# Two attention-and-FFN chunks, products of zeros between the real ones: adding them in chunk 1

## The chip, the core and the metric

The kernel runs on one core of one Trainium2 chip. The metric is the device time of the whole program in microseconds; the time before is the median of three runs. The profile shows one execution: for each engine when its instructions ran and what they waited for, and for TensorE (PE) also the clock that it was granted, 1.00 being full speed.

## The reference

Four batches of 768 tokens with 8 heads of 64 go through a sparse attention and then through a feed-forward block. In the attention a query sees the keys closer than 16 positions and, beside them, 24 block summaries: the maximum of 32 keys, and the mean of 32 values.

```python
k_sum = k.reshape(B, H, nb, block, D).max(axis=3)
v_sum = v.reshape(B, H, nb, block, D).mean(axis=3)
scores_l = scale * np.matmul(q, k.transpose(0, 1, 3, 2))     # masked: |i-j| < 16
scores_s = scale * np.einsum('bhsd,bhnd->bhsn', q, k_sum) + np.log(block)
a = softmax(concat([scores_l, scores_s]))                    # (written out in full there)
x = a @ concat([v, v_sum])                                   # heads side by side: (B, S, 512)
h = np.maximum(x @ w_in, 0.0)                                # 512 -> 1024
conv_out = sum over k of conv_w[k] * h shifted by k - 1      # three taps along the tokens
out = (h * sigmoid(conv_out)) @ w_out                        # 1024 -> 512
```

## The kernel before

**Chunks and units.** A chunk is half a batch, 384 tokens; there are eight, `c` = 0 to 7, and batch 0 is chunks 0 and 1. The feed-forward width of 1024 is cut into eight row blocks of 128. A unit `(c, u)` does row block `u` of chunk `c`, and with it a slice of the attention of the next chunk, so that attention and feed-forward share PE.

**The products, all on PE.** Attention: `pq` (L260, scores), `pt` (L308, transposing the weights), `xp` (L329, weights times values), `pv` (L234, one transpose for the value means). Feed-forward: `f1` (L404), 12 products of 384 or 386 columns for a row block, from three pairs of parts (`win_hi` with `xh`, `win_hi` with `xl`, `win_lo` with `xh`); and `f2` (L473), the last product. One `f2` tile is 128 tokens by 512 outputs; it adds up eight parts, `fc` = 0 to 7, of three products each (`wout_hi` with `ghi`, `wout_lo` with `ghi`, `wout_hi` with `glo`), in one PSUM bank. Then ScalarE (ACT) copies the bank out (`ob`, L482). The parts are `[fc]` lists that `work(c)` deals out over the units: chunk 1 gets the tiles (0,0) and (0,1), 16 parts, over its units 3 to 7 (`EARLY_AT` = 3).

**Behind a row block.** `gate_conv` takes the relu (ACT, L422) and the taps (ACT L425, VectorE (DVE) L434) from the bank of `f1`; `gate_mul` follows with tanh (ACT L451), the gating (DVE L452), `ghi` (ACT L455) and `glo` (GpSimd (POOL) L456). `f1` has three banks.

**Weights of the last product.** Each of the eight row blocks of `w_out` is decoded on ACT (L97) and DVE (L100, L101, L104), then ACT makes `wout_hi` (L127) and POOL makes `wout_lo` (L128). `OUT_AT` puts these splits into the units from (0,6) to (1,4).

**Products of zeros.** `idle` is a bf16 tile of zeros. `warm(where)` issues `WARM[where]` products of 512 columns of it into the PSUM tile `pw` (L78), whose values nobody reads. In chunk 0 that happens at the start, behind attention products and, with `after`, behind the last `f1` product of each unit (three each). `pw` has the tag `f2` with one buffer, so it holds the same bank as the tiles (b, 0), (b, 1) and so on of the last product: the first of them, (0,0), gets the bank when the last product into `pw` has been issued.

**Who sets the order.** From chunk 2 on PE's order is the order of the program (`manual_schedule`, with `ORDERED` = 2). In chunks 0 and 1 a planner sets it, on every engine: it plays the program through with estimated durations and issues on each engine, of what is ready, what stands first in the program. Work that stands later is pulled ahead where the planner sees the engine without other work. All queues run in the order so fixed.

Of the kernel before, what the change touches and what calls it, by code (L numbers as in the profile page):

```python
# [16 lines left out]
P = 128  # L17
# [12 lines left out]
NFC = DF // P  # L30
# [10 lines left out]
EARLY_IN = 2  # L41

OUT_AT = (6, 7, 8, 9, 10, 10, 11, 12)
WARM = {"start": 10, "pq0": 5, "pq1": 12, "pq2": 3, "pq3": 3, "tr": 2, "av": 3, "unit": 3}
EARLY_AT = 3
ORDERED = 2
NGROUP = NCHUNK * NP * 2
# [3 lines left out]
def attention_ffn(ctx, tc, qT, kT, vT, v4, w_in, cwT, w_out, mask8, ident_in, out):  # L51
    nc = tc.nc
# [18 lines left out]
    idle = cp.tile([P, 512], mybir.dt.bfloat16, name="idle")  # L71
# [3 lines left out]
    def warm(where, after=None):  # L75
        def go():
            for i in range(WARM.get(where, 0)):
                nc.tensor.matmul(pw, idle[:, :P], idle, start=True, stop=True)  # L78

        if after is None:  # L80
            go()
        else:
            with tc.issue_after(after):
                go()
# [28 lines left out]
    def split_in(fc, t):  # L113
        weights(t, flat(win_hi, fc), flat(win_lo, fc), f"i{fc}")

    def load_out(fc):
        t = sp.tile([P, 1024], U32, tag="stage", name=f"wo{fc}", bufs=2)
        nc.sync.dma_start(t, w_out[fc].bitcast(U32))
        return t

    def split_out(fc, t):
        weights(t, wout_hi[:, fc, :], wout_lo[:, fc, :], f"o{fc}")
# [18 lines left out]
    def ins(x):  # L141
        return getattr(x, "ins", x)
# [216 lines left out]
    def slot(j):  # L359

        if j % 2 == 0:
            n = j // 2 + 2
            if NP <= n < npair:
                load_k(*divmod(n, NP))
                load_vt(*divmod(n, NP))
            if NP <= j // 2 < npair:
                load_vm(*divmod(j // 2, NP))
            if j // 2 < npair:
                qk(*divmod(j // 2, NP))
        else:  # L370
            n = (j + 1) // 2
            if NP <= n + 1 < npair:
                load_q(*divmod(n + 1, NP))
            if n < npair:
                c, p = divmod(n, NP)
                if c:
                    vmean_pair(c, p)
                    load_v(c, p)
                prep_pair(c, p)

    def slot_t(j):
        if 0 <= j - DEPTH < NGROUP:
            tr(j - DEPTH)

    def slot_av(j):
        n = j - DEPTH - 2
        if n % 2 == 0 and 0 <= n < NGROUP:
            av(n // 2)
# [4 lines left out]
    def f1(c, fc, ccs):  # L393
        hf = c % 2
        n = CH + 2 * hf
        xh, xl = xT[c]
        if ccs[0] == 0:
            f1ps[(c, fc)] = ps.tile([P, 512], F32, tag="f1", name=f"f1_{c}_{fc}", bufs=3)
        ph = f1ps[(c, fc)]
        for cc in ccs:  # L400
            for m, (w, x) in enumerate(
                ((win_hi, xh), (win_hi, xl), (win_lo, xh))
            ):
                last = nc.tensor.matmul(  # L404
                    ph[:, :n],
                    w[:, fc, cc, :],
                    x[:, cc, :n],
                    start=(cc == 0 and m == 0),
                    stop=(cc == NCC - 1 and m == 2),
                )  # L410
        return last
# [3 lines left out]
    def gate_conv(c, fc):  # L415


        hf = c % 2
        n = CH + 2 * hf
        ng = CH - 1 + 2 * hf  # L420
        h = f1ps.pop((c, fc))
        nc.scalar.activation(h[:, :n], h[:, :n], AF.Relu)  # L422
        t = sp.tile([P, CH + 2], F32, tag="t", name=f"t{c}_{fc}", bufs=3)[:, :ng]
        if c in TAP_ACT:
            nc.scalar.activation(t, h[:, hf : hf + ng], AF.Copy, scale=cw[:, fc, 1:2])  # L425
        else:
            nc.vector.tensor_scalar(
                t, h[:, hf : hf + ng], cw[:, fc, 1:2], 1.0, ALU.mult, ALU.mult
            )
        for k in (0, 2):  # L430

            i0 = max(0, 1 - hf - k)
            i1 = min(ng, n - (hf + k - 1))
            nc.vector.scalar_tensor_tensor(  # L434
                t[:, i0:i1],
                h[:, hf + k - 1 + i0 : hf + k - 1 + i1],
                cw[:, fc, k : k + 1],
                t[:, i0:i1],
                ALU.mult,
                ALU.add,  # L440
            )
        held[(c, fc)] = h, t
# [19 lines left out]
    def f2(b, st, fcs, tag="f2", bufs=1):  # L462
        if fcs[0] == 0:
            f2ps[(b, st)] = ps.tile([P, 512], F32, tag=tag, name=f"f2_{b}_{st}", bufs=bufs)
        po = f2ps[(b, st)]
        ss = slice(st * P, (st + 1) * P)
        ghi, glo = gated["hi"], gated["lo"]
        for fc in fcs:
            contracted.add((b, st, fc))
            for m, (gx, w) in enumerate(  # L470
                ((ghi, wout_hi), (ghi, wout_lo), (glo, wout_hi))
            ):
                nc.tensor.matmul(  # L473
                    po,
                    gx[:, fc, ss],
                    w[:, fc, :],
                    start=(fc == 0 and m == 0),
                    stop=(fc == NFC - 1 and m == 2),
                )
        if fcs[-1] == NFC - 1:  # L480
            ob = sp.tile([P, DM], F32, tag="wu", name=f"ob{b}_{st}", bufs=3)
            nc.scalar.activation(ob, po, AF.Copy, scale=0.5)  # L482
            nc.scalar.dma_start(out[b, ss, :], ob)
# [71 lines left out]
    def rooms():  # L555
        gated["hi"] = cp.tile([P, NFC, S], F32R, name="ghi", tag="big_a")
        gated["lo"] = cp.tile([P, NFC, S], F32R, name="glo", tag="big_b")

    def gates(lag):

        while len(pending) > lag:
            c, fc = pending[0]
            b, hf = divmod(c, 2)
            old = (0, 1, 2) if hf == 0 else (2, 3, 4, 5)
            if b and not all((b - 1, st, fc) in contracted for st in old):
                return
            pending.pop(0)
            gate_mul(c, fc)

    def unit(c, u, pieces, together):  # L570


        j = 8 * (c + 1) + 1 + DEPTH + u
        last = c == NCHUNK - 1
        slot(j)
        if together:
            slot_av(j)
            slot_t(j)
        if c == 0 and u < 2:
            for fc in (4 + 2 * u, 5 + 2 * u):  # L580
                split_in(fc, raws[fc])
        if c == 0 and u == 2:
            rooms()
        gates(1)
        early = c == 0 and u < EARLY_IN
        if not early:
            f1(c, u, [0, 1])
        if not together:
            slot_t(j)
        done = f1(c, u, [3] if early else [2, 3])  # L590
        if c == 0:
            warm("unit", ins(done))
        gate_conv(c, u)
        pending.append((c, u))
        assert len(pending) <= 2
        if not together:
            slot_av(j)
        for x in pieces[u]:
            f2(*x)
        if last:  # L600
            gates(0)
        at = NFC * c + u
        for fc in range(NFC):
            if OUT_AT[fc] == at:
                split_out(fc, raws["o", fc])
        for fc in range(NFC):
            if OUT_AT[fc] == at + 1:
                raws["o", fc] = load_out(fc)

    for c in range(NCHUNK):  # L610
        pieces = work(c)
        if c < ORDERED:
            for u in range(NFC):
                unit(c, u, pieces, False)
        else:
            with tc.manual_schedule(engines={mybir.EngineType.PE}):
                for u in range(NFC):
                    unit(c, u, pieces, True)

    for pair in ((2, 3), (4, 5)):  # L620
        for fs in (range(NFC // 2), range(NFC // 2, NFC)):
            for st in pair:
                for fc in fs:
                    f2(B - 1, st, [fc], "f1" if st % 2 else "f2", 3 if st % 2 else 1)
# [55 lines left out]
```

## Time and profile before

| | us |
|---|---|
| three runs | 404.59, 408.15, 409.48 |
| median | 408.15 |
| the profiled execution, its own time | 408.03 |
| its span, first to last instruction | 406.2 |
| PE busy | 386.4 (95%) |
| DVE / ACT / POOL busy | 261.3 / 254.2 / 151.6 |
| mean granted clock of PE | 0.986 |

Between the span and the execution's own time lie 1.83 us that no instruction of the program fills. A busy share is the mean over very different stretches: chunk 0 begins after a stage of attention alone, chunk 1 is roughly the stretch from 80 to 129 us, chunk 7 ends near 381 us, and the last four tiles of the last product follow by themselves. PE works in a pipeline, so what one product costs is read from start to start, not from its duration.

### The profile page before, as it was taken

How to read it: one execution, taken by the hardware profiler on the slowest of the kernel's cores; microseconds unless marked ns; L12 is line 12 of the kernel's file. 1: busy time of each engine (PE TensorE's matmuls, PEld its weight loads, DVE VectorE, ACT ScalarE, POOL GpSimd, SP SyncE). 2: the span in 40 equal slices, each digit the busy share in tenths (PEclk: the TensorE clock that was granted, in tenths of full speed). 3: DMA queues.
4: the chain of work that ended last, by engine and by line, in shares of the span. 5: the costliest groups of instructions: out<-in, count | busy, mean ns of one | idle time of the engine just before them, and what ended most of it. 6: DMA issues, size and time to landing. Idle time of an engine off the chain costs nothing.

```text
span 406.2 us, 8829 instructions
## 1 busy us (share of the span) xinstructions
PE 386.4 (95%) x3164; PEld 319.5 (79%) x3173; DVE 261.3 (64%) x777; ACT 254.2 (63%) x806; POOL 151.6 (37%) x179
## 2 busy tenths in 40 slices
PE   7978869999799999999999999999999999999996
PEld 3546657886678888888888888888788888999884
DVE  4899789998965765668765456466565665556200
ACT  3664799998777677766565777756655654343211
POOL 2327464585953333322432333333332242222200
PEclk9999699999989999999999999999999999999999
DMA  8999863766966774646332344334220000000011
GB/s 290 327 361 211 230 177 115 248 202 192 252 162 205 235 217 123 190 145 192 78 92 78 80 111 112 104 96 117 67 63 28 27 2 26 26 27 26 28 52 52
DMA packets 60715, 54.47 MB, mean 134 GB/s; under 512 B 24640, under 2 KB 51328, under 8 KB 60672
## 3 DMA queue, kind: packets, MB, share of 16 engines
q1 hardware_dynamic: 56928, 47.19, 41.3%
q10 hardware_dynamic: 3744, 6.73, 4.5%
q8 instruction: 25, 0.41, 0.4%
q14 instruction: 18, 0.15, 0.1%
HBM read 45.55 MB, written 6.29 MB: 128 GB/s over the span
## 4 chain that ended last, share of the span: by engine, by line
PE 68%; ACT 11%; DVE 10%; DMA 3%; issue 3%; POOL 3%; SPq 0%; ACTq 0%; DVEq 0%; POOLq 0%
PE f L404 26%; PE f L473 26%; PE pq L260 5%; ACT a L288 5%; PE xp L329 4%; PE pt L308 4%; DVE t L434 3%; PE pw L78 2%; ACT t L451 1%; DMA kw<-kT 1%; DMA k_xh<-kT 1%; ACT f L422 1%; DVE t L452 1%; POOL wout_lo L128 1%; ACT t L425 1%
## 5 line engine op out<-in xcount | busy, mean ns | idle before, releaser
L456 POOL TENSOR_TENSOR glo<-t,ghi 128x383 fp32r<-128x383 f32 (+1 forms) x64 | 66.6, 1041 | 116.3 <-ACT ghi L455 111.8
L434 DVE SCALAR_TENSOR_TENSOR t<-f,cw,t 128x382 f32<-128x382 f32 (+3 forms) x128 | 78.8, 616 | 23.5 <-ACT t L425 20.7
L404 PE MATMUL f<-xh,win_hi 128*128 128x384 f32 (+1 forms) x256 | 93.0, 363 | 0.9 <-ACT win_hi L127 0.9
L404 PE MATMUL f<-xl,win_hi 128*128 128x384 f32 (+1 forms) x256 | 87.7, 343 | 0.0
L404 PE MATMUL f<-xh,win_lo 128*128 128x384 f32 (+1 forms) x256 | 86.9, 340 | 0.0
L473 PE MATMUL f<-wout_lo,ghi 128*128 128x512 f32 x192 | 76.1, 396 | 3.1 <-POOL wout_lo L128 3.1
L288 ACT ACTIVATE a<-a,nm 128x120 f32<-128x120 f32 x192 | 73.3, 384 | 9.1 <-DVE nm L278 8.8
L473 PE MATMUL f<-wout_hi,ghi 128*128 128x512 f32 x192 | 76.3, 398 | 0.2 <-ACT ob L482 0.2
L473 PE MATMUL f<-wout_hi,glo 128*128 128x512 f32 x192 | 75.1, 392 | 0.0
L451 ACT ACTIVATE t<-t 128x383 f32<-128x383 f32 (+1 forms) x64 | 33.6, 525 | 60.4 <-DVE t L434 59.3
L300 POOL TENSOR_TENSOR a<-a,sm 128x360 f32<-128x360 f32 x56 | 45.8, 839 | 64.4 <-DVE sm L297 36.5
L452 DVE SCALAR_TENSOR_TENSOR t<-t,f 128x383 f32<-128x383 f32 (+1 forms) x64 | 35.3, 552 | 28.2 <-ACT t L451 28.2
L404 PEld LDWEIGHTS f<-xh,win_hi 128*128 128x128 f32 x256 | 48.7, 190 | 3.6 <-issue 1.3
L404 PEld LDWEIGHTS f<-xl,win_hi 128*128 128x128 f32 x256 | 49.0, 191 | 0.9 <-issue 0.3
L404 PEld LDWEIGHTS f<-xh,win_lo 128*128 128x128 f32 x256 | 48.8, 191 | 0.2
L278 DVE CUSTOM_DVE_ANT_0 a<-pq,mask 128x120 f32<-128x120 f32 x192 | 42.7, 276 | 1.9 <-PE pq L260 1.9
L473 PEld LDWEIGHTS f<-wout_lo,ghi 128*128 128x128 f32 x192 | 36.3, 189 | 9.7 <-POOL wout_lo L128 4.1
L455 ACT CAST ghi<-t 128x383 fp32r<-128x383 f32 (+1 forms) x64 | 32.6, 509 | 16.6 <-DVE t L452 15.9
L473 PEld LDWEIGHTS f<-wout_hi,glo 128*128 128x128 f32 x192 | 36.2, 188 | 7.7
L473 PEld LDWEIGHTS f<-wout_hi,ghi 128*128 128x128 f32 x192 | 36.1, 188 | 7.3 <-issue 0.6
L308 PE MATMUL pt<-ident,a 128*120 128x128 f32 x192 | 34.0, 285 | 5.4 <-ACT aT L315 3.7
L260 PEld LDWEIGHTS pq<-kw,q 64*64 64x64 f32 x768 | 23.9, 134 | 18.6 <-issue 13.0
(59 smaller groups left out, 505.8 us busy)
## 6 DMA issues: line engine op xcount, KB each, us to landing
va<-v SPq DMA_DIRECT2D x32, 288.0 KB
kw<-kT SPq DMA_DIRECT2D x28, 288.0 KB
q<-qT SPq DMA_DIRECT2D x32, 192.0 KB
out_dram<-ob ACTq DMA_DIRECT2D x24, 256.0 KB
kT<-kT SPq DMA_DIRECT2D x12, 392.0 KB
vt<-vT SPq DMA_DIRECT2D x12, 384.0 KB
wo<-w_out SPq DMA_DIRECT2D x8, 512.0 KB
raw_a<-w_in SPq DMA_DIRECT2D x6, 512.0 KB
```

What stands on the lines that cost most here:

```text
L260: last = nc.tensor.matmul(pq[h][half * QB : (half + 1) * QB, i * NK : (i + 1) * NK], st["q"][r, blk * QB : (blk + 1) * QB], st["kw"][r, bl ...
L278: nc.vector.tensor_tensor_reduce(a[:, i, :], pq[h][:, i * NK : (i + 1) * NK], mask[:, hf, i, :], -0.125, 3.0e38, ALU.add, ALU.min, nm[:, h ...
L288: nc.scalar.activation(a[:, i, :], a[:, i, :], AF.Exp, bias=nm[:, h, i : i + 1], scale=-1.0, accum_out=sm[:, h, i : i + 1],)
L300: (nc.gpsimd if n >= NP else nc.vector).tensor_tensor(a, a, sm[:, h, :].unsqueeze(2).to_broadcast([P, 3, NK]), ALU.mult)
L308: last = nc.tensor.transpose(pt[:NK, i * P : (i + 1) * P], a[:, i, :], ident)
L404: last = nc.tensor.matmul(ph[:, :n], w[:, fc, cc, :], x[:, cc, :n], start=(cc == 0 and m == 0), stop=(cc == NCC - 1 and m == 2),)
L434: nc.vector.scalar_tensor_tensor(t[:, i0:i1], h[:, hf + k - 1 + i0 : hf + k - 1 + i1], cw[:, fc, k : k + 1], t[:, i0:i1], ALU.mult, ALU.add,)
L451: nc.scalar.activation(t, t, AF.Tanh, scale=0.5)
L452: nc.vector.scalar_tensor_tensor(t, t, 1.0, h[:, hf : hf + ng], ALU.add, ALU.mult)
L455: nc.scalar.copy(hi, t)
L456: nc.gpsimd.tensor_tensor(gated["lo"][:, fc, d0 : d0 + ng], t, hi.bitcast(F32), ALU.subtract)
L473: nc.tensor.matmul(po, gx[:, fc, ss], w[:, fc, :], start=(fc == 0 and m == 0), stop=(fc == NFC - 1 and m == 2),)
```

## The change

Two things are added, both on PE, and both change no value. Behind the last `f1` product of the units (1,0), (1,1) and (1,2), `warm("unit")` is now called as in chunk 0: three products of zeros into `pw` each, nine in all. And in `f2`, for the tiles (0,0) and (0,1), each part but the last is followed by two products of zeros that are added to the tile's own bank (`start=False, stop=False`): 7 parts of 2 tiles by 2, 28 in all. With the nine, `pw` is in use up to unit (1,2).

```diff
-WARM = {"start": 10, "pq0": 5, "pq1": 12, "pq2": 3, "pq3": 3, "tr": 2, "av": 3, "unit": 3}
+WARM = {"start": 10, "pq0": 5, "pq1": 12, "pq2": 3, "pq3": 3, "tr": 2, "av": 3, "unit": 3, "part": 2}
@@ f2, in the loop over the parts, behind the three products
+            if (b, st) in ((0, 0), (0, 1)) and fc < NFC - 1:
+
+                for _ in range(WARM["part"]):
+                    nc.tensor.matmul(po, idle[:, :P], idle, start=False, stop=False)
@@ unit
         done = f1(c, u, [3] if early else [2, 3])
-        if c == 0:
+        if c == 0 or (c == 1 and u < EARLY_AT):
             warm("unit", ins(done))
```

## The prediction

> **What bounds the kernel now.** I read the page's first two parts, then the granted clock over all of the span in stretches, then PE's waits in chunk 1, then the timeline of PE around the longest of them and the chain that leads to it. The page and the list of cores:
>
> ```profile
> core 0: 406.2 us, clock 0.986
> PE 386.4 (95%) x3164; PEld 319.5 (79%) x3173; DVE 261.3 (64%) x777; ACT 254.2 (63%) x806; POOL 151.6 (37%) x179
> PEclk9999699999989999999999999999999999999999
> ```
>
> PE is the bound as a whole, and its clock is below full in two slices only, the fifth and the twelfth. Stretches chosen around these two and around chunk 1 (columns: busy time of PE, weight loads, DVE, ACT, POOL with counts, the granted clock, DMA share, GB/s):
>
> ```profile
> 43.50:49.95 6.45, 6.45 (x28) 5.10 (x27) 5.16 (x19) 4.19 (x20) 2.43 (x3) 0.50 0.76 208
> 60.00:88.00 28.00, 27.79 (x285) 22.40 (x287) 26.47 (x80) 25.93 (x88) 16.59 (x21) 1.00 0.56 176
> 88.00:97.80 9.80, 9.80 (x75) 7.87 (x74) 8.60 (x19) 8.77 (x26) 6.75 (x7) 1.00 0.74 226
> 97.80:110.40 12.60, 9.37 (x64) 6.88 (x62) 12.60 (x32) 10.57 (x31) 9.67 (x9) 1.00 0.81 223
> 111.40:114.65 3.25, 3.25 (x25) 2.50 (x24) 1.25 (x4) 2.47 (x11) 0.20 (x1) 0.50 0.94 182
> 114.70:122.50 7.80, 7.64 (x72) 5.88 (x70) 5.75 (x21) 5.55 (x15) 5.23 (x5) 0.99 0.62 168
> 122.50:131.00 8.50, 8.50 (x46) 7.12 (x46) 4.91 (x9) 6.35 (x21) 3.79 (x5) 1.00 0.62 188
> 131.00:381.00 250.00, 248.18 (x2041) 217.70 (x2039) 151.70 (x448) 152.94 (x479) 80.77 (x99) 1.00 0.33 93
> ```
>
> From 60 to 97.8 us PE is full at full clock, and from 122.5 on it is full to the end. Between lies the only soft place of chunk 1: from 97.8 to 110.4 PE is idle for 12.60 - 9.37 = 3.23 us while DVE is busy throughout, and just behind it the clock stands at 0.50 for 3.25 us. What PE waits for there:
>
> ```profile
> PE f L473 <- POOL wout_lo L128: 3.1, 3, 2.4
> 107.40 0.40 PE L473 MATMUL f<-wout_hi,ghi 128*128 128x512 f32 x1
> 107.64 0.34 PE L404 MATMUL f<-xl,win_hi 128*128 128x386 f32 x1
> 110.41 0.50 PE L473 MATMUL f<-wout_lo,ghi 128*128 128x512 f32 x1 [2.44 <-POOL wout_lo L128]
> ```
>
> The sixth part of tile (0,0) stops PE for 2.44 us in its middle, between its first and its second product, until POOL has made the low half of that weight block. The chain that leads there:
>
> ```profile
> 89.50 2.31 PE f L404 x12
> 92.78 0.12 PE pv L234
> 94.02 0.58 ACT t L425
> 96.22 0.98 DVE wu_o L101
> 100.86 0.63 ACT wout_hi L127
> 104.74 1.98 POOL a L300 x2
> 108.67 1.69 POOL wout_lo L128
> ```
>
> It leaves PE behind the row block (1,2) and the transpose `pv`, and runs for 17 us over ACT, DVE and POOL. So products on PE between 93 and 107 us are not on the path, and what delays (1,2) or `pv` is.
>
> **The price of a product of zeros.** A unit of chunk 0 with three of them between `f1` and `pq`, and a place in chunk 1 where `pq` follows `f1` directly; then two products of a part in the dense stretch:
>
> ```profile
> 73.54 0.34 PE L404 MATMUL f<-xh,win_lo 128*128 128x384 f32 x1
> 73.72 0.82 PE L78 MATMUL pw<-idle 128*128 128x512 bf16 x3
> 74.47 0.85 PE L260 MATMUL pq<-kw,q 64*64 64x120 f32 x24
> ...
> 81.96 0.34 PE L404 MATMUL f<-xh,win_hi 128*128 128x386 f32 x1
> 82.22 0.63 PE L260 MATMUL pq<-kw,q 64*64 64x120 f32 x14
> ...
> 127.31 0.39 PE L473 MATMUL f<-wout_hi,ghi 128*128 128x512 f32 x1
> 127.54 0.40 PE L473 MATMUL f<-wout_lo,ghi 128*128 128x512 f32 x1
> ```
>
> From `f1` to `pq` it is 74.47 - 73.54 = 0.93 us with three and 82.22 - 81.96 = 0.26 without: 0.67 for three, 0.22 each. A real product of the same 512 columns follows the last in 0.23, so I take 0.225 also for those added to the tile's bank, which the trace of before does not have. That price has a floor of 0.22 and, if the change of weights between a part and its zeros broke the pipeline, a ceiling of their whole duration, about 0.39 as for the products beside them. Below nothing it can't be: a product holds PE. I take the low end because in the rows above zeros stand between real products and cost no more than that. All 37 cost 9 x 0.223 + 28 x 0.225 = 8.3 us of PE; the question is how much of it lies in idle time.
>
> **Nine behind the row blocks.** Those of (1,0) and (1,1) stand in the full stretch, ahead of (1,2): +1.34 us on the chain's start. There is something against it. The bank of `pw` passes to tile (0,0) only behind the zeros of (1,2), so the tile's first part can no longer run ahead of that row block, as it does now:
>
> ```profile
> 87.98 0.50 PE L473 MATMUL f<-wout_hi,ghi 128*128 128x512 f32 x1
> 88.88 0.62 PE L260 MATMUL pq<-kw,q 64*64 64x120 f32 x6
> 89.43 0.45 PE L404 MATMUL f<-xh,win_hi 128*128 128x386 f32 x1
> ...
> 92.29 0.50 PE L473 MATMUL f<-wout_hi,ghi 128*128 128x512 f32 x1
> 92.62 0.27 PE L234 MATMUL pv<-ident,vs 128*24 128x128 f32 x1
> ...
> 87.71 0.55 DVE L452 SCALAR_TENSOR_TENSOR t<-t,f 128x383 f32<-128x383 f32 x1
> ```
>
> That part takes 88.88 - 87.98 = 0.90 us there, and goes to a place behind (1,2), which is the third row block of 386 columns, the one that starts at 89.43. Whether (1,2) then starts 0.90 earlier depends on its bank: the gating of chunk 0's last block reads a bank of `f1` until 87.71 + 0.55 = 88.26 us, and with PE 1.34 later that is no hindrance. So (1,2) ends 1.34 - 0.90 = 0.44 later. Its own three zeros, issued behind its last product and ahead of `pv`, add 0.67: the chain is 1.1 us late. The bounds: 0.4 (the planner puts `pv` ahead of them, or the first product of the second part, 92.62 - 92.29 = 0.33, moves as well) and 2.0 (nothing gained from the moved part).
>
> **Ten behind the first five parts of tile (0,0).** 10 x 0.225 = 2.25 us between 93 and 107, beside the chain. What PE has to do before the sixth part's second product grows by 9 x 0.223 + 2.25 = 4.26 us, the moved part being the same work in another place. The idle time that takes it is 3.23 us and the 1.1 by which POOL is later, together 4.33. It just fits: PE reaches 111.5 instead of 110.4 with almost no stop, and the delay stays 1.1. If the cover were gone (POOL not later, 3.23 alone), it would be 4.26 - 3.23 = 1.03, the same.
>
> **Four behind the sixth and seventh part, fourteen in tile (0,1).** Behind 110.4 us PE has 7.80 - 7.64 = 0.16 us of idle and then none. The tile (0,1), eight parts of three products, runs in the full stretch, as the chain shows:
>
> ```profile
> 122.66 2.84 PE f L473 x12
> 126.58 2.95 PE f L473 x12
> ```
>
> So 18 x 0.225 = 4.05 us on the path, and at a price of 0.39 it would be 7.0. Nothing waits on another engine there for which they would be early; the next chunk's products queue behind them.
>
> **The clock.** If the idle time is filled, the half clock of 3.25 us goes, and the work in it takes half: -1.63 us. The trace has the pattern twice, and here is the row of the other place, just ahead of 43.50 us:
>
> ```profile
> 42.15 0.83 PE L260 MATMUL pq<-kw,q 64*64 64x120 f32 x12 [1.94 <-issue]
> ```
>
> Idle for 1.94 us, then 6.45 us at 0.50; idle for 2.44 us, then 3.25 at 0.50. The early one is ahead of the change and stays. [...]
>
> **The sum.** 1.1 + 4.05 - 1.63 = +3.5 us against the profiled execution's own 408.03 us, 0.12 below the median of the runs, with the 1.83 us outside its span unchanged: 411.5 us. Behind 131 us I let it through whole; there the chain goes over PE and DMA and buffers that PE frees, which shift with PE.
>
> **Rivals.**
>
> The half clock stays (18 in 100). For it: the zeros come in pairs of 0.45 us and the stop is inside a part, where none stand; if the planner puts other work elsewhere, 2 us of stop remain at the same place. Against it: the balance of 4.26 against 4.33 above. Time: 408.03 + 1.1 + 4.05 = 413.2. [...]
>
> Part of it is lost in idle time further on (15 in 100). From 131 to 381 us PE is idle for 250.00 - 248.18 = 1.82 us. If these stops end at times that do not move with PE, they swallow up to 1.8: 409.7. Against it: the longest step of the chain there is a load that begins when PE has done with a buffer, and moves with PE:
>
> ```profile
> 231.50 0.84 PE pq L260 x24
> 232.40 5.29 DMA kw<-kT
> ```
>
>
> Slower beyond the bound (12 in 100): the bank's handover decides. If (1,2) can't use the 0.90 us that the first part leaves, because its bank or its inputs come no earlier, a hole opens on PE at 88 us, the chain is late by 2.0, the POOL chain moves along with PE instead of covering it, and all 37 products lie on the path: 8.3 + 0.9 = 9.2, half clock kept, 417.2. It decides from the point where the gating that ends at 88.26 now ends more than 1.3 us later than that. Against it: this gating is behind chunk 0's last block, ahead of the first added product.
>
> The planner's new order helps (8 in 100): the parts of (0,0) start later, DVE and ACT get row block (1,2) earlier instead of later, and the 17 us chain shortens by the 0.90 of the moved part, with the ten zeros in the idle time: 408.03 - 0.9 + 4.05 - 1.63 = 409.6, and if the order hides half of the 4.05 too, 407.5.
>
> **How the numbers follow.** My forecast, 47 in 100, has its own range: 0.4 to 2.0 for the chain gives 410.8 to 412.4, and the zeros' price at 0.39 up to 414.5. Runs of the same program lie between 404.59 and 409.48, that is 3.4 below the profiled execution and 1.5 above. The range that holds it 8 times in 10: 405.0 (between the 407.5 of the last rival and that less 3.4 for a favourable run) to 416.5, leaving out most of the slow rival. About 2% is what a measurement of this kernel can tell from no change: 400.0 to 416.3 around the median. Faster needs 8 us, and the idle time and the half clock of chunk 1 hold 3.23 + 1.63 = 4.9 with nothing paid: 3 in 100. Slower takes most of the third rival's 12: 9 in 100. The rest, 88, is the same.
>
> **What would show it.** The group L78 has nine records more, and a new line in `f2` up to 28. In the stretch that answers to 97.8 to 110.4, PE idle below 1 us and no wait on `wout_lo` above 1; the clock 1.00 from 50 us to the last slice; tile (0,0)'s first product behind row block (1,2) and its zeros; the tile (0,1) taking some 3.1 us more than now; chunk 2 beginning 3 to 4 us later, and the same distance at the end. I am wrong in the cover if the wait on `wout_lo` is still 2 us long with the zeros on either side of it, in the price if zeros in the tile's bank start more than 0.3 us apart, and in the order if row block (1,2) is not the first to run ahead of tile (0,0) or if stops appear in places where there are none now.

## The result, and the profile after

The changed kernel takes 411.60 us (median of 14 runs, 409.94 to 415.16), the kernel before 408.01 (14 runs, 404.51 to 410.07). The ratio is 1.011, with a 95% interval of 1.0081 to 1.0140: about 4.5 us slower (3.3 to 5.7), clear of noise and inside 2%. The forecast was 411.5. The traces show that several of the steps that led there were wrong, and that their errors cancelled.

The profiled execution of the changed kernel took 412.74 us, with a span of 411.0. The busy line and the clock line of its page, and the row of its cores:

```profile
core 0: 411.0 us, clock 0.990
PE 392.5 (96%) x3210; PEld 319.8 (78%) x3210; DVE 261.5 (64%) x777; ACT 254.4 (62%) x806; POOL 150.3 (37%) x179
PEclk9999699999999999999999999999999999999999
```

PE is busy for 6.1 us more than before, DVE and ACT for the same, POOL for 1.3 us less, and the low clock of the twelfth slice is gone. The weight loads grow by the 37 that were added (3173 to 3210), the records of products by 46: nine of chunk 0's products of zeros have no record in the profile of before. The products of zeros in the tiles' bank are all there; here is their group:

```profile
L483 PE MATMUL f<-idle x28: 379/384/393, 99.7 to 133.7; 128*128 128x512 bf16 x28
```

To see where the time lies I measure chunk 1 on PE, from the first product of 386 columns to the first of 384 after it, which is chunk 2's first. Those two rows, of before and then of the changed kernel:

```profile
79.93 0.45 PE L404 MATMUL f<-xh,win_hi 128*128 128x386 f32 x1
129.61 0.42 PE L404 MATMUL f<-xh,win_hi 128*128 128x384 f32 x1
```

```profile
81.59 0.45 PE L404 MATMUL f<-xh,win_hi 128*128 128x386 f32 x1
134.85 0.43 PE L404 MATMUL f<-xh,win_hi 128*128 128x384 f32 x1
```

Chunk 1 is 49.68 us long before and 53.26 after, +3.58. Ahead of it the changed kernel's profile is already 1.66 us late, though the order on PE up to there is the same but for those nine records; this is the draw of one execution (last section). Behind it the two run alike: from chunk 2's first product to the last copy out of a bank it is 402.51 - 129.61 = 272.90 us before and 407.31 - 134.85 = 272.46 after. 1.66 + 3.58 - 0.44 = 4.8, the difference of the spans. So what the change costs lies in chunk 1, and 0.44 us of it comes back behind.

The timeline of the changed kernel around the stop on `wout_lo`:

```profile
98.14 0.34 PE L404 MATMUL f<-xh,win_lo 128*128 128x386 f32 x1
98.41 0.56 PE L329 MATMUL xp<-aT,va 120*64 120x64 f32 x10
98.90 0.50 PE L473 MATMUL f<-wout_hi,ghi 128*128 128x512 f32 x1
...
108.36 0.43 PE L260 MATMUL pq<-kw,q 64*64 64x120 f32 x6
110.75 0.50 PE L473 MATMUL f<-wout_lo,ghi 128*128 128x512 f32 x1 [1.95 <-POOL wout_lo L128]
111.09 0.40 PE L473 MATMUL f<-wout_hi,glo 128*128 128x512 f32 x1
111.32 0.61 PE L483 MATMUL f<-idle 128*128 128x512 bf16 x2
111.86 0.63 PE L260 MATMUL pq<-kw,q 64*64 64x120 f32 x14
112.42 0.44 PE L404 MATMUL f<-xh,win_hi 128*128 128x386 f32 x1
...
119.48 0.50 PE L473 MATMUL f<-wout_lo,ghi 128*128 128x512 f32 x1 [0.85 <-POOL wout_lo L128]
```

Tile (0,0) starts at 98.90, behind row block (1,3), one row block later than the handover of the bank demands. But the stop is still 1.95 us long, and a second of 0.85 has grown where 0.16 was. Row block (1,5), of which most stood ahead of the stop before (105.86 to 107.64), now starts at 112.42, behind it. And the clock behind the stop is full although PE stood still for 1.95 us.

### The profile page after: what moved, and what is told of

Read it like the earlier page. It is cut to its first block, busy times and chain, and to the rows that moved or that the text cites. A ratio compares the mean times of both kernels' runs of the same rounds, so it can differ in the third digit from the quotient of the medians.

```text
span 411.0 us, 8910 instructions
## 1 busy us (share of the span) xinstructions
PE 392.5 (96%) x3210; PEld 319.8 (78%) x3210; DVE 261.5 (64%) x777; ACT 254.4 (62%) x806; POOL 150.3 (37%) x179
## 4 chain that ended last, share of the span: by engine, by line
PE 66%; ACT 14%; DVE 12%; POOL 3%; issue 3%; DMA 2%; ACTq 0%; DVEq 0%; POOLq 0%
PE f L473 25%; PE f L404 24%; ACT a L288 6%; PE pq L260 5%; PE pt L308 4%; PE xp L329 4%; DVE t L434 3%; PE pw L78 3%; ACT t L451 2%; DVE t L452 1%; ACT t L425 1%; ACT ghi L455 1%; DMA k_xh<-kT 1%; ACT f L422 1%; DMA va<-v 1%
## 5 line engine op out<-in xcount | busy, mean ns | idle before, releaser
L473 PE MATMUL f<-wout_hi,ghi 128*128 128x512 f32 x192 | 77.4, 403 | 0.2 <-ACT wout_hi L127 0.2
L300 POOL TENSOR_TENSOR a<-a,sm 128x360 f32<-128x360 f32 x56 | 44.8, 820 | 70.3 <-DVE sm L297 36.6
L350 DVE TENSOR_TENSOR xl<-xp,xh 128x384 fp32r<-128x384 f32 x32 | 17.7, 554 | 31.6 <-ACT xh L349 31.4
```

The lines of the kernel that those rows point to most:

```text
L300: (nc.gpsimd if n >= NP else nc.vector).tensor_tensor(a, a, sm[:, h, :].unsqueeze(2).to_broadcast([P, 3, NK]), ALU.mult)
L473: nc.tensor.matmul(po, gx[:, fc, ss], w[:, fc, :], start=(fc == 0 and m == 0), stop=(fc == NFC - 1 and m == 2),)
```

## The experiments

Each kernel is the one before with only the edit that is shown. Beside the ratio I give chunk 1's length in the profile, measured as above, for it is free of what happens ahead of it. Where a half clock fell into it, I say so: the same program (the single product of zeros, below) was profiled once with and once without one, and chunk 1 was 48.85 and 47.57 us long, so I take 1.28 as its cost. With it taken out, chunk 1 of the kernel before is 49.68 - 1.28 = 48.40 us at full clock, and the changed kernel's 53.26 is 4.86 more. The 1.28 comes from one pair of profiles. The timed runs of the kernel before put it a little higher: straight lines through the three sets that the experiments were compared with give 1.3, 1.4 and 1.6 us for each 3.41 us of half clock more. With 1.6 the base would be 48.1 and every difference to it 0.3 larger; differences between two profiles without a half clock in chunk 1 don't depend on it.

**Only the nine behind the row blocks.**

```diff
-        if c == 0:
+        if c == 0 or (c == 1 and u < EARLY_AT):
             warm("unit", ins(done))
```

> Only the nine products of zeros behind the row blocks (1,0) to (1,2), none in the bank of the tiles. Theory of the record (the chain over DVE and POOL is 1.1 us late, the stop on wout_lo stays long and the half clock with it): +1.1 us on before. Rival, read from the trace of the changed kernel (all zeros lie on the path, and the new order that comes with the bank's later handover pays about 2 us back, the pq products standing in fewer pieces): +2.0 less 2, so 0 within 1 us, with tile (0,0) starting behind row block (1,3).

Ratio 1.0023 (0.9986 to 1.0061). Chunk 1 is 49.53 us with a half clock in it, so 48.25 without: -0.15. The stop:

```profile
110.03 0.51 PE L473 MATMUL f<-wout_lo,ghi 128*128 128x512 f32 x1 [2.83 <-POOL wout_lo L128]
```

The stop is long, as the theory of the record has it, but the chain that ends it is not late: from chunk 1's start at 80.07 to the end of the stop it is 29.96 us, against 110.41 - 79.93 = 30.48 before. Nine products, 2.0 us of PE, show no cost in chunk 1 (the ratio's interval allows up to 2.5 us). Much of it is paid by the new order: ahead of the stop stand the same 62 score products as before, but in other pieces (14, 2, 2, 16, 4, 8 and 16 instead of 14, 12, 6, 6, 2, 4, 12 and 6), and PE is busy with them for 4.05 us instead of 5.15.

**Only the 28 in the tiles' bank, and each tile's 14 alone.** (The diff is of the run with tile (0,1); that with tile (0,0) has `(0, 0)`, that with both has the condition of the change.)

```diff
+            if (b, st) == (0, 1) and fc < NFC - 1:
+                for _ in range(WARM["part"]):
+                    nc.tensor.matmul(po, idle[:, :P], idle, start=False, stop=False)
```

> Only the 28 products of zeros in the bank of the tiles (0,0) and (0,1), none behind the row blocks, so the bank of pw passes on as in the kernel before. Theory of the record (ten lie in the stop, 18 on the path, the half clock goes): 4.05 - 1.63 = +2.4 us. Rival (all 28 on the path, nothing paid back): +6.3 us, or +4.7 if the half clock goes.

> Only the 14 products of zeros in the bank of tile (0,1). Both theories have these in a stretch where PE is full: 14 x 0.225 = +3.15 us on before. Much less would say that PE's order or its later stops take them up; up to 5.5 that a product of zeros behind a real part costs its whole duration of 0.39.

> Only the 14 products of zeros in the bank of tile (0,0): ten ahead of the stop of 2.44 us, four behind it. Theory of the record (the ten lie in the stop): stop 0.2 us, +0.9 on the path, half clock gone, -0.7 us on before. Rival (the planner counts the zeros as work and puts products of row block (1,5) behind the stop in their stead, as the traces of the run with all 28 and of the changed kernel show; the stop stays about 2 us): chunk 1, clock aside, about +1.9, the same as all 28 less those of tile (0,1), and fewer than 68 f1 products ahead of the stop's end.

| zeros in the bank of | ratio | chunk 1, full clock | against 48.40 |
|---|---|---|---|
| both tiles, 28 | 1.0102 (1.0063 to 1.0140) | 53.43 | +5.03 |
| tile (0,1), 14 | 1.0111 (1.0076 to 1.0147) | 51.53 | +3.13 |
| tile (0,0), 14 | 1.0062 (1.0020 to 1.0104) | 50.23 | +1.83 |

Tile (0,1)'s are paid in full: 14 x 0.225 = 3.15 was forecast. Without the base it is much the same: the run with all 28 is 53.43 - 50.23 = 3.20 longer than the run with tile (0,0)'s alone. The timed runs don't show this order: the ratio with (0,1)'s 14 is no smaller than with all 28, and the three intervals overlap. The lengths of chunk 1 are from one profile each. The trace of the run with tile (0,1), chunk 1's two ends and the stop:

```profile
82.30 0.45 PE L404 MATMUL f<-xh,win_hi 128*128 128x386 f32 x1
112.77 0.50 PE L473 MATMUL f<-wout_lo,ghi 128*128 128x512 f32 x1 [2.43 <-POOL wout_lo L128]
133.83 0.43 PE L404 MATMUL f<-xh,win_hi 128*128 128x384 f32 x1
```

The stop comes 30.47 us behind chunk 1's start and is 2.43 long, as before; no zeros of this kernel stand ahead of it. And yet no half clock follows it. So the half clock's absence after the change proves nothing for the zeros.

Tile (0,0)'s were to lie in the stop. They do not. Its two stops, and the `f1` products (columns: stretch, its length, PE's busy time with count, weight loads with count, clock, DMA) from chunk 1's start to the end of the first stop:

```profile
111.51 0.50 PE L473 MATMUL f<-wout_lo,ghi 128*128 128x512 f32 x1 [2.05 <-POOL wout_lo L128]
120.62 0.50 PE L473 MATMUL f<-wout_lo,ghi 128*128 128x512 f32 x1 [0.99 <-POOL wout_lo L128]
81.18:111.51 30.33, 13.86 (x66) 11.18 (x66) 1.00 0.76 212
```

The same stretch before, and in the changed kernel, each with the row for all products below it (here DVE, ACT and POOL follow the weight loads):

```profile
79.93:110.41 30.48, 14.47 (x68) 11.69 (x68) 1.00 0.74 214
79.93:110.41 30.48, 27.25 (x222) 21.61 (x221) 28.94 (x74) 26.77 (x79) 24.05 (x23) 1.00 0.74 214
```

```profile
81.59:110.75 29.16, 12.79 (x60) 10.20 (x60) 1.00 0.77 215
81.59:110.75 29.16, 26.98 (x210) 19.69 (x209) 28.39 (x67) 25.45 (x74) 23.01 (x22) 1.00 0.77 215
```

The stop ends at the same distance from the start (30.33 and 30.48 us). But ahead of it stand 66 `f1` products instead of 68, in the changed kernel 60 of them, and 48 `xp` instead of 54: the planner reckons with the zeros as with any work and lets them push real products behind the stop, where PE has no room. The score products ahead of the stop are as many as before (62) but take 4.44 us instead of 5.15. So the stop shrinks only from 2.44 to 2.05. Behind it come the four last zeros (0.9 us), what was pushed back, and the second stop. For the changed kernel, whose second stop is 0.85 long, the chain shows how it arises:

```profile
111.93 0.62 PE pq L260 x14
112.86 1.25 ACT a L288 x6
116.67 1.52 POOL a L300 x2
118.20 1.24 POOL wout_lo L128
```

The score products `pq`, put behind the first stop, delay the softmax on ACT and POOL's part of it, and these stand ahead of the last `wout_lo` on POOL. With tile (0,0)'s zeros alone the score products are not behind the stop; there the chain leaves PE over one transpose `pt`, but ends in the same two steps on POOL.

**A single product of zeros**, for the handover of the bank alone. Run twice.

```diff
-WARM = {..., "unit": 3}
+WARM = {..., "unit": 3, "last": 1}
-        if c == 0:
-            warm("unit", ins(done))
+        if c == 0 or (c == 1 and u == EARLY_AT - 1):
+            warm("unit" if c == 0 else "last", ins(done))
```

> A single product of zeros, behind row block (1,2): it costs 0.22 us and keeps the bank of pw from tile (0,0) as the nine do. Theory of the record: the tile's first part moves out of the way of (1,2), chain 0.9 earlier, so -0.7 us. Rival (the new order itself pays back): about -2 us, pq in fewer pieces, stops on wout_lo as long as before. If a hole opens at the place of the first part, as the slow rival of the record has it: +1.

> The run with the single product of zeros behind row block (1,2), once more: its chunk 1 was 48.85 us with a half clock of 3.41 us in it, 47.2 without, 0.85 under before. If that is the order's gain: a ratio near 0.997 again. If it was the draw of the clock: a ratio near 1.000.

Ratios 0.9969 (0.9933 to 1.0005) and 0.9957 (0.9922 to 0.9991): 0.3 and 0.4% under before, the first not clear of no change. Chunk 1 is 48.85 us with a half clock and 47.57 without, 0.83 less than 48.40. The ratios amount to 1.3 and 1.8 us, but part of that can be the clock: the mean granted clock of these runs is 0.992 both times, against 0.988 before. A stretch of 3.41 us at half clock is 0.004 of the mean, so by the price above the difference is worth some 1 us. Whether the edit raised the clock or the draw did is not shown. Rows of the first run and of the second:

```profile
82.67 0.45 PE L404 MATMUL f<-xh,win_hi 128*128 128x386 f32 x1
89.96 1.46 PE L260 MATMUL pq<-kw,q 64*64 64x120 f32 x22
131.52 0.42 PE L404 MATMUL f<-xh,win_hi 128*128 128x384 f32 x1
```

```profile
81.34 0.45 PE L404 MATMUL f<-xh,win_hi 128*128 128x386 f32 x1
128.91 0.42 PE L404 MATMUL f<-xh,win_hi 128*128 128x384 f32 x1
```

With the first part out of the way, 22 score products run in one piece ahead of (1,2); before, they came in pieces of 12, 6 and 6 around the parts. In chunk 1 the gain is of the size that was expected (-0.7, and -0.83 measured). No hole opened at its place, so the record's slow rival falls.

**The handover one unit later**, with the single product behind (1,3): the same edit with `u == EARLY_AT`.

> The single product of zeros one unit later, behind row block (1,3), so the bank of pw passes to tile (0,0) later still. If a later start of the tile is what helps: at or under the ratio of the single product behind (1,2), 0.997. If the parts then crowd behind the stop: chunk 1 longer by 1 us or more.

Ratio 0.9977 (0.9942 to 1.0011), chunk 1 47.56 us. The same as behind (1,2).

**Zeros inside the stop.**

```diff
+                if (b, st, fc, m) == (0, 0, 5, 0):
+                    for _ in range(8):
+                        nc.tensor.matmul(po, idle[:, :P], idle, start=False, stop=False)
```

> Eight products of zeros in one piece inside the sixth part of tile (0,0), between its first and its second product, where PE stops now; nothing else of the change. If zeros inside the stop are free: stop 2.44 - 1.8 = 0.6 us, chunk 1 as long as before at full clock (48.05 us), no half clock behind it, 0 to -0.5 us. If the planner moves other products behind the stop in their stead: the stop stays near 2 and chunk 1 is 1 to 1.8 us longer.

Ratio 1.0010 (0.9977 to 1.0043), chunk 1 48.98 us, +0.58.

```profile
111.57 0.50 PE L473 MATMUL f<-wout_lo,ghi 128*128 128x512 f32 x1 [0.85 <-POOL wout_lo L128]
118.73 0.50 PE L473 MATMUL f<-wout_lo,ghi 128*128 128x512 f32 x1 [0.87 <-POOL wout_lo L128]
```

Put into the stop itself, 1.8 us of zeros do shorten it, to 0.85, but a third of their cost stays on chunk 1, and the second stop grows to 0.87. That third, too, is read against the base of 48.40. With five of them and the single product behind (1,2):

> The single product of zeros behind (1,2), and five inside the sixth part of tile (0,0), where PE stops. [...] If the planner moves other work for them: 1.000.

Ratio 0.9993 (0.9960 to 1.0027), chunk 1 47.37 us at full clock. The profile is the second shortest, the runs are not: no gain to be seen over the single product. The stop is 1.51 us long, and the mean granted clock of the runs is 0.989, no higher than before (0.988): no gain from the clock either.

**What the stop is worth.** The product that waits becomes one of zeros; the low half of that weight block is left out of this one tile.

```diff
+                none = (b, st, fc, m) == (0, 0, 5, 1)
                 nc.tensor.matmul(
                     po,
-                    gx[:, fc, ss],
-                    w[:, fc, :],
+                    idle[:, :P] if none else gx[:, fc, ss],
+                    idle if none else w[:, fc, :],
```

> What the stop itself is worth: before, but the second product of the sixth part of tile (0,0), the one that waits 2.44 us for POOL, is a product of zeros of the same length, so the low half of that weight block is left out of that one tile. If the stop is on the path: chunk 1 shorter by up to 2.4 us at full clock (48.05 down to 45.7), and no half clock behind it, -3 us on the median at most. If PE only waits for the next thing (the next part's wout_lo, the gating of the row blocks): chunk 1 shorter by less than 1.

Ratio 0.9938 (0.9903 to 0.9974), 2.5 us; chunk 1 46.84 us, -1.56. The next part's `wout_lo` then ends a stop of 0.99:

```profile
113.04 0.51 PE L474 MATMUL f<-wout_lo,ghi 128*128 128x512 f32 x1 [0.99 <-POOL wout_lo L128]
```

So much are this stop and the clock behind it worth: 1.56 us in chunk 1, and 1.1 to 4.0 us by the ratio's interval. The change spends 8.3 us of zeros, by the record's price.

**The same means at two earlier stops.**

```diff
+        if (c, p) == (1, 2):
+            warm("gap2", ins(last))          # behind the scores: 10
...
-            f1(0, fc, [cc])
+            done = f1(0, fc, [cc])
+    warm("gap1", ins(done))                  # behind the early products: 8
```

> The same means at other stops: before plus eight products of zeros behind the first row blocks' early products (ahead of the stop of 1.94 us at 42 us) and ten behind the scores of pair 2 of chunk 1 (ahead of the stop of 2.73 us at 58 us); nothing in chunk 1. If they lie in the stops and the half clock of 6.45 us at 43.5 goes: up to -3.2 us. If the planner moves other work behind the stops, or PE waits for neither: up to +4.0.

> As the run before it (18 products of zeros at the two early stops) with the single product of zeros behind row block (1,2), whose run alone came 0.3% under before. If the two add up: early's result less 1 us. If the order it gives depends on what went before: no difference to early.

Ratios 1.0124 (1.0076 to 1.0172) and 1.0157 (1.0111 to 1.0203): slower by 5.1 us where 4.0 was the most expected. With the handover it is no faster; the two intervals overlap. The stop of 2.73 us at 58 us did fill, with zeros from 55.63 on; from 50 to 72 us no stop is longer than 0.34. The stop at 42 us did not, it grew:

```profile
46.31 1.47 PE L260 MATMUL pq<-kw,q 64*64 64x120 f32 x12 [3.21 <-DMA q<-qT]
```

It now waits for a load of `q`. The issue of that load before, and in this run:

```profile
40.48 0.51 SPq L185 DMA_DIRECT2D q<-qT  x1
```

```profile
42.81 0.51 SPq L185 DMA_DIRECT2D q<-qT  x1
```

The load of `kw` ahead of it in the queue waits for 24 score products, and these start at 40.52 instead of 38.19, right behind seven recorded zeros that take 1.6 us. So in this run the zeros, which stand ahead of the products on which the queue waits, delay the load by 42.81 - 40.48 = 2.33 us, and the stop with it.

## Why the prediction was right, and where it was not

The total was right and the direction too. The terms, all for chunk 1 at full clock; each measured one comes from the run with that part alone:

| step of the prediction | forecast | measured |
|---|---|---|
| nine behind the row blocks, chain late | +1.1 | -0.15 |
| ten in tile (0,0), in the stop, and four behind it (0.9) | +0.9 | +1.83 |
| fourteen in tile (0,1), on the path | +3.15 | +3.13 |
| half clock behind the stop | -1.63 | none on the mean |
| sum | +3.5 | +4.81 |

In chunk 1 the parts add up: 4.81 against 4.86 for all of them together. In the timed runs they don't: the three ratios give 0.9, 2.5 and 4.5 us, 8.0 in sum, where all together give 4.5. Each is uncertain by some 1.5 us; behind chunk 1 the two profiles with one tile's zeros take 0.70 and 0.42 us longer than before, which is a part; the rest stays open. With the 0.44 that the profile gives back behind chunk 1, 4.86 - 0.44 = 4.4 us, and the ratio says 4.5.

**The price of a product of zeros** held: 3.13 / 14 = 0.224 us, and 3.20 / 14 = 0.229 without the base, on the bank of a tile as on `pw`. In the changed kernel the parts of tile (0,1) with their zeros follow each other every 1.14 us, five products of 0.228. The upper bound of 0.39 was their duration, not their cost.

**The nine.** The handover was right: with the single product (1,2) starts 8.67 us behind chunk 1's start instead of 9.50, and the stop ends 0.8 earlier. What failed is the balance, "(1,2) ends 1.34 - 0.90 = 0.44 later", and with it the 1.1 of the chain. I moved one part and kept the rest of the order; the planner moved the score products too. Of the 18 that stood between row block (1,1) and (1,2) before, the changed kernel has 4 there and the others behind (1,2). So (1,2) starts at 90.88, which is 9.29 us behind chunk 1's start, against 9.50 before, with six zeros ahead of it. Nor does (1,2) or `pv` alone set the chain: `pv` comes 0.2 us later than before, counted from chunk 1's start, and yet the stop ends 1.3 earlier (29.16 for 30.48). The order on POOL changed too: the copy of `kw`, 0.44 us long, that stood ahead of `wout_lo` before (106.73) stands there no more.

**The ten in the stop.** "What PE has to do before the sixth part's second product grows by ... 4.26" is the step that failed. It did not grow: PE is busy for 27.25 us ahead of the stop's end before and for 26.98 in the changed kernel. The zeros came in, but `f1`, `xp` and `pq` together take 3.8 us less there (1.68, 0.44 and 1.70). I had counted the zeros into an order that would not stay. The cover was there for work put at the place of the stop (eight inside it shortened it by 1.59), not for work ahead of it. What I named as the sign of this error, a wait still 2 us long with zeros on either side, is what the trace shows.

**The clock.** The half clock is absent in the changed kernel's profile, but the zeros did not remove it: it is absent also with zeros in tile (0,1) alone, behind the same stop of 2.43. Over the timed runs the mean granted clock is 0.988 with the change, and 0.988 to 0.989 in the three sets of before. What one execution of before lost was booked as lost in all; the first rival, in which the half clock stays and 2 us of the stop remain, was the better account of what happens, though its time, 413.2, is further from 411.6 than the forecast.

Of the four errors two were too dear (the nine by 1.25, the time behind chunk 1 by 0.44) and two too cheap (tile (0,0) by 0.93, the clock by 1.63). Together the forecast was 0.9 too cheap: it is low against the ratio's 4.5 us and just right against the difference of the medians, 3.6. That 411.5 stands so close to 411.6 owes much to errors that cancelled and to the draw of the clock.

## What to carry to other kernels

In chunk 1 work of no use, put into a planned order, was not laid into the gap: it took the place of real work, and that went behind the gap. Count what stands ahead of a stop before and after (here 68 and 60 `f1` products) rather than the stop's length, and put a filler, if any, directly ahead of the instruction that waits. Where one execution shows a slow clock, ask how often it falls there before a gain is booked for its going. And a buffer's handover, changed in passing, can be worth more than what was meant: one product of zeros for 0.22 us made chunk 1 shorter by 0.8 us.

## What the runs showed of the hardware

**When the clock falls.** The stop on `wout_lo` in chunk 1, and the half clock on record behind it, in six profiles:

| profile | stop, us | half clock behind it |
|---|---|---|
| before | 2.44 | 111.39 to 114.80 |
| the nine | 2.83 | 111.74 to 115.15 |
| the single product, first run | 2.44 | 112.37 to 115.78 |
| the single product, second run | 1.98 | none |
| tile (0,1) alone | 2.43 | none |
| the changed kernel | 1.95 | none |

The rows of the three stretches at half clock (columns as in the prediction's stretches), and one at full clock with tile (0,1) alone, whose stop ends in it at 112.77:

```profile
111.39:114.80 3.41, 3.41 (x26) 2.57 (x25) 1.41 (x4) 2.62 (x11) 0.21 (x1) 0.50 0.94 185
```

```profile
111.74:115.15 3.41, 3.41 (x30) 2.58 (x28) 1.87 (x4) 3.41 (x14) 0.00 (x0) 0.50 1.05 211
```

```profile
112.37:115.78 3.41, 3.41 (x23) 2.77 (x24) 1.12 (x8) 0.88 (x4) 1.16 (x1) 0.50 1.20 222
```

```profile
111.95:115.36 3.41, 2.59 (x28) 2.11 (x28) 1.97 (x11) 1.42 (x5) 2.02 (x2) 1.00 1.19 211
```

The length of the stop does not tell the two cases apart: 2.44 us before have a half clock behind them and 2.43 with tile (0,1) alone have none, and one program, the single product, has it in one execution and not in the other. The stop of 2.73 us at 58 us, before, has none behind it either: from 49.95 to 111.38 the clock is 1.00. What decides it these profiles do not show, nor what decides how long it lasts: 3.41 us in the three rows, and before, from 43.13 to 49.95, 6.82 us, with PE busy in all of them.

**The clock at the start.** The changed kernel's profile is late from the first products on. The five zeros behind the first score products, of before and after:

```profile
7.17 1.25 PE L78 MATMUL pw<-idle 128*128 128x512 bf16 x5
```

```profile
8.13 2.32 PE L78 MATMUL pw<-idle 128*128 128x512 bf16 x5
```

They take 1.25 and 2.32 us, in the second case near double, though the clock column has 1.00 for both places. The trace's own record of the clock begins at 5.58 us in the first case and at 10.59 in the second, so the slow five lie ahead of it, and what clock they had is not shown. The changed kernel's mean of 0.990 takes that time as full, so these two profiles are best compared from a point behind it.
